# Another plan of tiles, other tap shares and another instruction order in a local-attention and MoE kernel

## The chip, the cores and the metric

The kernel runs on one core of a Trainium2 chip. The metric is device time in microseconds of one execution. Engines: TensorE (PE; PEld is its weight load), VectorE (DVE), ScalarE (ACT), GpSimd (POOL), and SyncE (SP), which only issues DMAs here.

## The reference

The input is `x` (8 x 3584 tokens of 192 numbers) and a weight generator of 8 heads with 7 taps per token. Each token's output of the first part is a softmax-weighted sum of itself and the six tokens before it; the second part routes each of the 28,672 tokens to one of 8 experts and applies that expert's two-layer network.

```python
w = softmax(weight_gen, over the 7 taps)
x1 = einsum('bshk,bskhg->bshg', w, windows_of_7(x_pad))      # attention, 8 heads of 24
logits = x1 @ w_gate                                         # 8 experts
e = argmax(logits)
for each expert e:                                           # tokens of that expert
    h  = relu(x1[mask] @ w1[e])                              # 192 -> 1024
    ye = h @ w2[e]                                           # 1024 -> 192
    out[mask] = softmax(logits)[e] * sigmoid(x1 @ w_output_gate)[e] * ye
```

## The kernel before, in words

**Units.** The tokens are worked in 32 units of 896 (128 partitions x 7). For each unit the front half loads `x` and `w` (`load_steps`, line 651), makes the softmax of the taps (`softmax_steps`, 676), forms the seven products x times w and adds them, scales the sum and splits it into two f16 parts (`sum_steps`, 822), transposes it (a DMA transpose into `gt` from unit 5 on), takes the gate's logits on PE, finds each token's expert and its place within that expert's rows (rank matmuls with `upper` and `ones`, line 905), and scatters the unit's 896 rows into `srtd` in DRAM, sorted by expert: seven indirect DMAs on POOL's queue (`place_steps`, 970).

**Taps.** `TAPS(u)` (1380) gives the first n of the seven products to POOL and the rest to VectorE. Units below `PE_U` = 6 always take `PRO_G` = 4, and PE adds the products up; from unit 6 on `SHARES` decides, or the pattern `POOL`, and VectorE adds the products up in PSUM.

**Rounds and tiles.** `plan_rounds` (28) fixes beforehand how many tiles each unit's round asks for. It counts the rows that have arrived, holds some of them back, and cuts the rest into tiles of T rows: `n = max(0, -(-(left - keep - HOLD(T)) // T))`, at most as the list `EARLY` or `SIZES` says; T is 512 but for the units in `EARLY`. On the chip a round finds for each tile an expert with T sorted rows. The last unit takes all that is left in tiles of 512, 256 and 128 rows. Rows are held back because no expert may yet have T rows of its own.

**A tile's work.** `tile_steps` (1119) waits until a round is filed, that is until all scatters of its units have been issued and are counted as landed, and calls `tile_load` (1141): on SP's queue a load of `meta`, a DMA transpose of the rows into `xT`, and the expert's weights into `wa` (two DMAs) and `wb`. At most `AHEAD` = 2 loaded tiles wait before the last round. `gemm_steps` (1265) then works beats on PE: two of a tile's units of the first matmul (`gemm1_unit`, for 512 rows five matmuls of 512 columns each), and one group of 128 rows of the second (`gemm2_group`, 24 matmuls of 192 columns). ACT and VectorE empty each first-matmul unit (`evac_steps`: `hh`, `hl`), ACT the second one (`out_steps`: `sc` once per tile, `ys`), and POOL scatters `ys` to the output by an indirect DMA per group.

**What sets the order.** Each engine runs its instructions in the order in which the program emits them. `Order.step` (118) emits them by a model: each chain of steps has a time at which its inputs are thought ready, and the chain that can go on first is taken, ties by rank (`RANK_...`, only compared with one another). The model's constants stand at the end: `LAT`, `LAT_S`, `LAT_P`, `LAT_T`, `LAT_R` (from the scan of a unit's ranks to its matmul), `LANDED` (behind a DMA's end), `SLACK`, `SMALL`, `WBX` (when `wb` counts as free again). `FAVOUR` takes tenths of a microsecond off one named chain. The constants change no data, only the emitted order.

**Stirring.** `stir` (502) emits dummy matmuls of 256 columns before a planned gap of PE of at least `STIR[0]` us, `STIR[1]` times the gap in length; it needs a bank of the early sums, which units 0 to 5 use.

Of the kernel before, what the change touches and what calls it, by code (L numbers as in the profile page):

```python
# [27 lines left out]
def plan_rounds(units, every, size):  # L28

    left, rounds = 0, {}  # L30
    for u in range(units):
        left += size
        last = u == units - 1
        if u not in every and not last:
            continue
        subs = []
        for T, keep in SIZES(u, last):
            n = max(0, -(-(left - keep - HOLD(T)) // T))
            while n > 0:
                k = min(n, 8)  # L40
                subs.append((T, k))
                left -= k * T
                n -= k
        if last:
            subs.append((128, (left + NE * TAILK) // 128))
        rounds[u] = subs
    return rounds
# [20 lines left out]
class Chain:  # L68


    def __init__(self, gen, rank, t, engine):
        self.gen, self.rank, self.t, self.engine, self.gate = gen, rank, t, engine, None
        self.favour, self.label = 0.0, ""
        self.slack = EAGER[1] if len(rank) > 1 and rank[0] in EAGER[2] and rank[1] < EAGER[0] else SLACK

# [8 lines left out]
class Order:  # L84
# [7 lines left out]
    def add(self, gen, rank, engine, t=None):  # L92
        c = Chain(gen, rank, self.cur.t if t is None else t, engine)
        c.label = label(gen)
        c.favour = FAVOUR.get(c.label, 0.0)
        self.chains.append(c)
# [60 lines left out]
class Queue:  # L157
# [12 lines left out]
    def __getattr__(self, name):  # L170
        f = getattr(self.engine, name)

        def call(*args, **kwargs):
# [6 lines left out]
            if own is not None:  # L180
                done = self.order.ring.land(self.issued - issue + ARRIVE, own)
                if name == "dma_start_transpose":
                    self.issued = max(self.issued, done - BACK)
                self.moved = max(self.moved, done)
                c.t = max(c.t, done + LANDED)
            return r
# [4 lines left out]
class Paced:  # L191
# [8 lines left out]
    def __getattr__(self, name):  # L200
        f = getattr(self.engine, name)

        def call(*args, **kwargs):
# [4 lines left out]
            if own is not None:  # L208
# [6 lines left out]
                if scatter:  # L215
                    self.landed = self.order.ring.land(self.t - own + 1.6, 0.262) + LANDED
                    held = False
                if held:
                    self.order.port = self.t
                c.t = max(c.t, self.t + self.after)  # L220
                self.order.close(self, args, kwargs, self.t + (LAT_P if self.after == 0.0 else self.after))
            return r
# [29 lines left out]
def vector_cost(name, args, kwargs):  # L252
# [5 lines left out]
    if name == "memset":  # L258
        return 0.03 + (n / 960.0 if n > 8 else 0.0)
    return SMALL + n / 960.0  # L260

# [45 lines left out]
def kernel(ctx: ExitStack, tc: tile.TileContext, x, wg, wgate, wogate, w1, w2, cst, out):  # L307
    nc = tc.nc
    od = Order()
    V = Paced(od, nc.vector, vector_cost, holds=two_in_sbuf)  # L310
# [59 lines left out]
    ps = pp.tile([P, 4096], F32, name="ps")  # L370
    tr_free = [(0.0, ps[:, at : at + 192].bitcast(F16)) for at in TURNS]

# [30 lines left out]
    U = {u: {} for u in range(-RT, NU + 3)}  # L403
# [178 lines left out]
    def weight_steps(stg):  # L582

        for e in range(NE):
# [7 lines left out]
            SP.dma_start(out=st2.rearrange("p (c d) -> p c d", d=D), in_=w2[e].rearrange("(c p) d -> p c d", p=P))  # L592
            od.add(split_steps(e, st1, st2), (RANK_W, e), S)
            if 3 < e < 7:
# [56 lines left out]
    def load_steps():  # L651
        for u in range(1, NU):
            od.named(f"load {u}")
            od.cur.rank = (RANK_X if u <= X_EARLY else RANK_A, -1)
            yield from take(w_free, SP)
            w_load(u)
            U[u]["wt"] = od.cur.t
            od.cur.t = od.now
            od.add(softmax_steps(u), (RANK_A, u, 0), V, U[u]["wt"])
            yield from take(x_free, SP)  # L660
            if u >= XN:
                yield SP, lambda: "zero" in U[u - XN + 1]
            x_load(u)
            U[u]["xt"] = od.cur.t
            od.cur.t = od.now
# [10 lines left out]
    def softmax_steps(u):  # L676

        w4 = wloads[u]
        mxb = f_mx.unsqueeze(2).broadcast_to([P, NV, K])
        yield from take(mx_free, V)  # L680
        V.tensor_reduce(out=f_mx, in_=w4, axis=AX, op=ALU.max)
        yield V
        V.tensor_tensor(out=w4, in0=w4, in1=mxb, op=ALU.subtract)
        yield S
        S.activation(w4, w4, AF.Exp)
        yield V
        V.tensor_reduce(out=f_mx, in_=w4, axis=AX, op=ALU.add)
        yield V
        V.tensor_scalar(f_mx, f_mx, 1e-9, None, op0=ALU.add)
        yield V  # L690
        V.reciprocal(out=f_mx, in_=f_mx)
        yield V

        n = len(TAPS(u)[0])
        V.tensor_tensor(out=w4[:, :, 0:n], in0=w4[:, :, 0:n], in1=f_mx.unsqueeze(2).broadcast_to([P, NV, n]), op=ALU.mult)
        yield V
        U[u]["gw"], U[u]["pool"] = od.cur.t, True
        _, at = yield from take(tw_free, V)
        tw = ps[:, at : at + NV * (K - n)].rearrange("p (v k) -> p v k", k=K - n)
        V.tensor_tensor(out=tw, in0=w4[:, :, n:K], in1=f_mx.unsqueeze(2).broadcast_to([P, NV, K - n]), op=ALU.mult)  # L700
        U[u]["tw"], U[u]["tw_at"], U[u]["tw_k"] = tw, at, n
        mx_free.append(od.cur.t)
        U[u]["wt"] = od.cur.t
        U[u]["soft"] = True
# [40 lines left out]
    def acc_steps(u, taps):  # L745
# [8 lines left out]
        while own or left:  # L754
            yield V, lambda: own or gp
            if own and not (n and gp and gp[0][2] <= od.now + SLACK):
                k = own.pop(0)
# [37 lines left out]
    def add_steps(u, t, tag, kind):  # L795
# [9 lines left out]
        for lo in (0, 512, 1024):  # L805
            hi = min(lo + 512, NV * GD)
            T_.matmul(d["sum"][:, lo:hi], lhsT=cf[:, 0:128], rhs=flat[:, lo:hi], start=(n == 0), stop=(n == K - 1 - PAIRS), skip_group_check=True)
        tap_free[tag].append((od.cur.t + LAT_P, kind))
        if n == 0:
# [3 lines left out]
        if n == K - 1 - PAIRS:  # L813
            d["total"] = d["sum"][:, 0 : NV * GD].rearrange("p (a b) -> p a b", b=GD)
            od.add(sum_steps(u), (RANK_B, u), S, T_.t + LAT_P)

# [5 lines left out]
    def sum_steps(u):  # L822
# [40 lines left out]
        else:  # L863
            od.cur.t += LAT_T
            for j0 in range(0, JS, 2):
# [34 lines left out]
        V.tensor_tensor_scan(out=p3e.rearrange("p e j -> p (e j)"), data0=segs, data1=ohe.rearrange("p e j -> p (e j)"), initial=0.0, op0=ALU.mult, op1=ALU.add)  # L900
        od.cur.t += LAT_R
        yield T_
# [24 lines left out]
    def turn_steps(u, rt, gt, copied):  # L927
        for j in range(JS):
            _, pt = yield from take(tr_free, T_)
            for k in range(3):  # L930
                T_.transpose(out=pt[:, k * 128 : (k + 1) * 128], in_=rt[:, j, k * 128 : (k + 1) * 128], identity=ident)
            od.add(copy_steps(gt[:, j], pt, copied, j), (RANK_B, u), S, T_.t + LAT_P)

# [185 lines left out]
    def tile_steps():  # L1119

        while "all" not in state or queue:
            yield SP, lambda: queue and state["weights"] == NE and len(ahead) < (LATE if "all" in state else AHEAD)
            yield from take(xt_free, SP)
            _, ka = yield from take(wa_free, SP)
            _, kb = yield from take(wb_free, SP)
            T, ti, i, pads, ready, u = queue[0]
            if ready > od.now:
                od.cur.t = ready
                yield SP
            queue.pop(0)  # L1130
            if pads is not None:
                for e in range(NE):
                    row = SP.value_load(pads[0:1, e : e + 1], min_val=0, max_val=DUMMY - P)
                    scattered(SP.dma_start(out=srtd[bass.ds(row, P), :], in_=pad), u)
            d = tile_load(state["t"], T, ti, i, ([n for v, n in state["writers"] if v <= u], [n for v, n in state["writers"] if v > u]), ka, kb)
            d["ready"] = od.cur.t
            state["t"] += 1
            ahead.append(d)
            od.cur.t = od.now
# [17 lines left out]
    def gemm1_unit(hp, d, u, at):  # L1157
# [5 lines left out]
        for i in range(nf):  # L1163
            f = u * nf + i
            b3 = 2048 + f * P
            for q, (wo, k) in enumerate(((f * P, 0), (1024 + f * P, 0), (f * P, 2), (b3, 1), (b3 + 1024, 1))):
                T_.matmul(ps[:, at + i * T : at + (i + 1) * T], lhsT=wa[:, wo : wo + P], rhs=xT[:, k, 0:T], start=(q == 0), stop=(q == 4), skip_group_check=True)
        od.add(evac_steps(d, ps[:, at : at + nf * T], hh[:, 0 : nf * T], hl[:, 0 : nf * T], at, u), (RANK_H,), S, T_.t + LAT_P)

# [9 lines left out]
    def gemm2_group(d, g, at):  # L1179
# [15 lines left out]
        if g == d["G"] - 1:  # L1195
            wb_free.append((T_.t + WBX, d["kb"]))
        od.add(out_steps(d, g, py, at), (RANK_Y,), S, T_.t + LAT_P)

# [121 lines left out]
    with tc.tile_pool(name="stg", bufs=STG, reuse_waits="tile") as stg:  # L1320
        stg_sq = stg
        od.add(weight_steps(stg), (RANK_W, 0), SP)
        while state["weights"] < NE:
# [22 lines left out]
    left = nc.values_load(state["left"][0:1, 0:1], min_val=0, max_val=N // P + NE)  # L1346
# [3 lines left out]
    with tc.For_i(0, left, 1):  # L1350
# [8 lines left out]
        d = tile_load(state["t"], P, ti, 0, ([], []), more, "wb")  # L1359
# [24 lines left out]


RANK_H, RANK_Y, RANK_C, RANK_R, RANK_B, RANK_A, RANK_G = 1, 0, 2, 3, 4, 5, 6
HOLD = lambda T: 6 * T
TAILK = 79
RANK_W = 4.5
LAT = 0.0756  # L1390
LAT_S = 0.2324
LAT_P = 0.3614
LAT_T = 1.8143
LOCK = True
ARRIVE = 1.9478
LANDED = 0.5447
LAT_R = 1.1028
SLACK = 0.0352
SCATTER = 0.987
SMALL = 0.0762  # L1400
EAGER = 0, 0.2, (2, 3, 4)
BACK = 1.0
TURNS = (1536,)
LEAD = 3.3869
STG = 4
# [10 lines left out]
XB = 4  # L1416
MB = 8
PRO_G = 4
POOL = (5,5,4)
SHARES = {18: 5, 11: 4, 28: 4, 20: 4}  # L1420
FAVOUR = {}
PE_U = 6
STIR = 0.8, 0.5
GIVE = 1
RANK_X = 2.5
X_EARLY = 3
RANK_GATE = 4.5
FIRST_G = ()
DEFER = 4
WBX = 3.3548  # L1430
PAIRS = 0
TURN_SP = True
GT = 1
TR_U = 5
EARLY = {2: ((256, 0),), 4: ((384, 0),), 5: ((384, 0),), 6: ((384, 0),)}
EVERY = {*range(99)}
MANUAL = ("SP", "DVE", "PE", "Activation", "Pool")

# [17 lines left out]
```

## Time and profile before

| | us |
|---|---|
| median of 3 runs | 1220.73 (1212.9, 1220.73, 1223.78) |
| the profiled execution | 1223.71 |
| span of its instructions | 1222.0 |
| mean granted TensorE clock | 0.978 of full |
| TensorE busy | 1120.0 |
| VectorE busy | 955.9 |
| POOL busy | 841.5 |
| ScalarE busy | 616.6 |

The span is the time from the first to the last instruction of one execution. The trace names instructions by what they write and read: `gap` and `vap`, `vt` are products of taps on POOL and on VectorE, `srtd<-rt,posi` is a scatter of a unit's rows, `out_dram<-ys,meta` one of results, `ps<-xT,wa` the first matmul of a tile, `ps<-wb,hh` and `ps<-wb,hl` the second, `ps<-gm,gt` the logits. Line 207 is a helper's line that nearly all instructions share; SPq is SyncE's queue.

### The profile page before, as it was taken

How to read it: one execution, taken by the hardware profiler on the slowest of the kernel's cores; microseconds unless marked ns; L12 is line 12 of the kernel's file. 1: busy time of each engine (PE TensorE's matmuls, PEld its weight loads, DVE VectorE, ACT ScalarE, POOL GpSimd, SP SyncE). 2: the span in 40 equal slices, each digit the busy share in tenths (PEclk: the TensorE clock that was granted, in tenths of full speed). 3: DMA queues.
4: the chain of work that ended last, by engine and by line, in shares of the span. 5: the costliest groups of instructions: out<-in, count | busy, mean ns of one | idle time of the engine just before them, and what ended most of it. 6: DMA issues, size and time to landing. Idle time of an engine off the chain costs nothing.

```text
span 1222.0 us, 27128 instructions
## 1 busy us (share of the span) xinstructions
PE 1120.0 (92%) x9693; PEld 812.1 (66%) x9693; DVE 955.9 (78%) x1874; ACT 616.6 (50%) x1300; POOL 841.5 (69%) x620
## 2 busy tenths in 40 slices
PE   8987686899979999999999998899999999999897
PEld 4544375677657666666666666676666666798697
DVE  7999696999999979998999989899998653333231
ACT  4986553455555545455555544455544434434342
POOL 6678783777898868887888877678888554322122
PEclk9999898999989999999999999899999999999999
DMA  8989699998697979799799969887979696599992
GB/s 280 285 276 299 194 287 268 215 270 235 172 264 176 260 225 232 164 250 233 192 244 249 253 163 246 235 212 197 236 193 195 192 270 196 165 292 244 321 292 84
DMA packets 294952, 282.77 MB, mean 231 GB/s; under 512 B 229222, under 2 KB 254423, under 8 KB 294816
## 3 DMA queue, kind: packets, MB, share of 16 engines
q1 hardware_dynamic: 272976, 236.54, 73.0%
q0 software_dynamic: 21696, 44.30, 12.5%
q8 instruction: 76, 1.25, 0.4%
q14 instruction: 60, 0.49, 0.1%
q10 hardware_dynamic: 144, 0.20, 0.1%
HBM read 174.77 MB, written 60.28 MB: 192 GB/s over the span
## 4 chain that ended last, share of the span: by engine, by line
PE 58%; DVE 17%; DMA 9%; issue 8%; POOL 5%; ACT 1%; SPq 1%; another core or an unknown queue 0%; POOLq 0%; DVEq 0%; ACTq 0%
PE ps L207 58%; DVE ps L207 9%; DVE hl L207 4%; DMA wa<-wd 4%; POOL srtd L207 3%; DMA srtd<-rt,posi 2%; POOL gap L207 1%; DVE vt L207 1%; SPq L175 1%; DMA gt<-rt 1%; DMA meta<-srtd 1%; DVE rt L207 1%; POOL out_dram L207 1%; DVE lz L207 1%; DMA w<-in_wg_dram 1%
## 5 line engine op out<-in xcount | busy, mean ns | idle before, releaser
L207 PE MATMUL ps<-xT,wa 128*128 128x512 f16 (+3 forms) x2440 | 491.1, 350 | 42.5 <-DMA wa<-wd 12.8
L207 PE MATMUL ps<-wb,hh 128*128 128x192 f16 x3648 | 473.5, 247 | 8.2 <-ACT ys L207 4.4
L207 PE MATMUL ps<-wb,hl 128*128 128x192 f16 x1824 | 450.1, 247 | 1.4 <-issue 1.4
L207 DVE SCALAR_TENSOR_TENSOR hl<-ps,hh 128x512 f16<-128x512 f32 (+1 forms) x470 | 305.2, 666 | 172.0 <-ACT hh L207 124.0
L207 POOL TENSOR_TENSOR gap<-x,w 128x1344 f32<-128x1344 f32 x145 | 379.4, 2624 | 43.2 <-issue 14.8
L207 POOL DMA_INDIRECT out_dram<-ys,meta x220 | 218.4, 993 | 243.2 <-ACT ys L207 176.1
L207 PEld LDWEIGHTS <-wa 128*128 128x128 f16 x2440 | 226.8, 99 | 229.0 <-issue 47.7
L207 PEld LDWEIGHTS <-hh 128*128 128x128 f16 x3648 | 332.5, 98 | 53.7 <-issue 15.9
L207 ACT ACTIVATE hh<-ps 128x512 f16<-128x512 f32 (+1 forms) x470 | 267.7, 582 | 177.6 <-PE ps L207 147.9
L207 POOL DMA_INDIRECT srtd<-rt,posi x224 | 230.2, 1028 | 85.2 <-issue 57.8
L207 ACT ACTIVATE ys<-ps,sc 128x192 f32<-128x192 f32 x228 | 95.8, 420 | 288.4 <-PE ps L207 180.1
L207 DVE TENSOR_TENSOR ps<-ps,gap 128x1344 f32<-128x1344 f32 x121 | 187.9, 1553 | 0.4
L207 PEld LDWEIGHTS <-hl 128*128 128x128 f16 x1824 | 179.3, 98 | 0.9 <-issue 0.6
L207 DVE SCALAR_TENSOR_TENSOR rt<-ps,sx,rt 128x448 f16<-128x448 f32 x64 | 57.6, 910 | 7.4 <-DMA srtd<-rt,posi 2.5
L207 PE MATMUL ps<-xT,late 128*128 128x128 f16 (+2 forms) x560 | 59.9, 263 | 3.7 <-DMA late<-wd 3.7
L207 PE MATMUL ps<-gap,cf 128*128 128x512 f32 x144 | 60.7, 559 | 0.0
L207 DVE TENSOR_TENSOR ps<-ps,vt 128x1344 f32<-128x1344 f32 x35 | 54.4, 1555 | 0.0
L207 DVE TENSOR_TENSOR vt<-x,ps 128x1344 f32<-128x1344 f32 x35 | 54.1, 1545 | 0.1
L207 PEld LDWEIGHTS <-late 128*128 128x128 f16 x560 | 40.2, 98 | 16.5 <-DMA late<-wd 3.9
L207 ACT ACTIVATE rt<-ps 128x1344 bf16<-128x1344 f32 x32 | 41.3, 1291 | 17.2 <-DVE ps L207 9.5
L207 ACT ACTIVATE rt<-ps,sx 128x1344 f16<-128x1344 f32 x32 | 44.2, 1380 | 11.4 <-DVE sx L207 8.2
L207 PE MATMUL ps<-gm,gt 128*128 128x32 f16 x672 | 28.1, 177 | 20.1 <-ACT gt L207 10.4
(121 smaller groups left out, 809.2 us busy)
## 6 DMA issues: line engine op xcount, KB each, us to landing
wb<-wd SPq DMA_DIRECT2D x75, 768.5 KB
wa<-wd SPq DMA_DIRECT2D x61, 768.0 KB
x<-in_x_dram SPq DMA_DIRECT2D x32, 672.0 KB
late<-wd SPq DMA_DIRECT2D x14, 768.0 KB
wa<-wd SPq DMA_DIRECT2D x61, 128.0 KB
w<-in_wg_dram SPq DMA_DIRECT2D x32, 196.0 KB
wd<-wpb SPq DMA_DIRECT2D x8, 768.5 KB
st<-in_w_dram SPq DMA_DIRECT2D x8, 768.0 KB
```

Source lines behind the costliest of these rows:

```text
L175: r = f(*args, **kwargs)
L207: r = f(*args, **kwargs)
```

## The change

Three functions get one edit each. `plan_rounds` takes the held rows from a table, `load_steps` and `tile_steps` get an added time that is zero. All else is constants: the table of held rows (2816 in place of 3072 for 512-row tiles, 1408 in place of 1536 for 256), the tap shares, the ranks and model constants, two favours, the stirring, and an entry for unit 3 in `EARLY`.

```diff
-            n = max(0, -(-(left - keep - HOLD(T)) // T))
+            n = max(0, -(-(left - keep - HOLDS[T]) // T))
...
-            od.add(softmax_steps(u), (RANK_A, u, 0), V, U[u]["wt"])
+            od.add(softmax_steps(u), (RANK_A, u, 0), V, U[u]["wt"] + (W_LATE if u > PE_U else 0.0))
...
-            d["ready"] = od.cur.t
+            d["ready"] = od.cur.t + T_LATE
...
-HOLD = lambda T: 6 * T
+HOLDS = {128: 768, 256: 1408, 384: 2304, 512: 2816}
 TAILK = 79
-RANK_W = 4.5
+RANK_W = 4.718
 LAT = 0.0756
 LAT_S = 0.2324
-LAT_P = 0.3614
-LAT_T = 1.8143
+LAT_P = 0.384
+LAT_T = 1.85
 LOCK = True
 ARRIVE = 1.9478
-LANDED = 0.5447
-LAT_R = 1.1028
-SLACK = 0.0352
+LANDED = 0.434
+LAT_R = 0.851
+SLACK = 0.038
 SCATTER = 0.987
-SMALL = 0.0762
+SMALL = 0.073
 EAGER = 0, 0.2, (2, 3, 4)
 BACK = 1.0
+W_LATE = 0
+T_LATE = 0.0
...
-POOL = (5,5,4)
-SHARES = {18: 5, 11: 4, 28: 4, 20: 4}
-FAVOUR = {}
+POOL = (5, 5, 5, 4)
+SHARES = {11: 4, 28: 5, 20: 5, 2: 3, 4: 4, 29: 5, 6: 5, 23: 4, 1: 3, 24: 5, 27: 5, 9: 5, 0: 3}
+FAVOUR = {'evac 21 2': 0.4, 'exp 19': -0.1}
 PE_U = 6
-STIR = 0.8, 0.5
+STIR = (0.37, 0.49)
 GIVE = 1
-RANK_X = 2.5
+RANK_X = 2.124
 X_EARLY = 3
-RANK_GATE = 4.5
+RANK_GATE = 4.275
 FIRST_G = ()
 DEFER = 4
-WBX = 3.3548
+WBX = 3.58
...
-EARLY = {2: ((256, 0),), 4: ((384, 0),), 5: ((384, 0),), 6: ((384, 0),)}
+EARLY = {2: ((256, 0),), 4: ((384, 0),), 5: ((384, 0),), 6: ((384, 0),), 3: ((384, 0),)}
```

## Rows read from the trace of the kernel before

**Rows 1.** The page, busy time of the engines; the chain's shares by engine.
```profile
PE 1120.0 (92%) x9693; PEld 812.1 (66%) x9693; DVE 955.9 (78%) x1874; ACT 616.6 (50%) x1300; POOL 841.5 (69%) x620
...
PE 58%; DVE 17%; DMA 9%; issue 8%; POOL 5%; ACT 1%; SPq 1%; another core or an unknown queue 0%; POOLq 0%; DVEq 0%; ACTq 0%
```

**Rows 2.** Busy time by stretch: us, engines (instructions), granted clock, DMA share, GB/s.
```profile
320.00:520.00 200.00, 185.54 (x1588) 129.58 (x1586) 186.06 (x346) 101.32 (x219) 168.25 (x120) 0.97 0.85 218
520.00:690.00 170.00, 163.23 (x1412) 115.98 (x1411) 157.01 (x319) 92.12 (x198) 145.60 (x103) 0.99 0.90 235
690.00:1010.00 320.00, 299.27 (x2560) 209.88 (x2558) 271.52 (x560) 155.45 (x341) 237.79 (x186) 0.98 0.86 217
1010.00:1146.00 136.00, 131.94 (x1411) 110.84 (x1408) 44.38 (x65) 54.05 (x111) 40.51 (x42) 1.00 0.81 230
...
343.00:349.00 6.00, 0.32 (x5) 0.22 (x4) 5.80 (x20) 1.83 (x7) 5.63 (x4) 0.70 1.05 279
866.00:928.00 62.00, 60.01 (x507) 42.33 (x505) 58.36 (x110) 32.25 (x71) 54.46 (x39) 1.00 0.84 206
```

**Rows 3.** The chain before 349 us; SP's queue from 315 us (start, us, what).
```profile
335.50 1.01 POOL out_dram L207
...
343.55 5.29 DMA wa<-wd
...
315.46 0.40 SPq L175 DMA_DIRECT2D meta<-srtd  x1
...
319.61 8.00 SPq L175 DMA_TRANSPOSE gt<-rt  x1
```

**Rows 4.** PE in order of time, from 348 and from 659 us (start, us, what [idle before]).
```profile
348.89 3.97 PE L207 MATMUL ps<-xT,wa 128*128 128x512 f16 x10 [5.68 <-DMA wa<-wd]
...
659.93 2.32 PE L207 MATMUL ps<-xT,wa 128*128 128x512 f16 x10
...
664.07 2.32 PE L207 MATMUL ps<-xT,wa 128*128 128x512 f16 x10
```

**Rows 5.** Loads issued and first scales done, counted from 0 to four moments (ns; first, last start).
```profile
L175 SPq DMA_DIRECT2D meta<-srtd x15: 111/398/423, 143.7 to 340.9; - x15
...
L207 ACT ACTIVATE sc<-meta,wb x15: 278/287/311, 164.2 to 372.2; 128x3 f32<-128x3 f32 x7, 128x2 f32<-128x2 f32 x5, 128x4 f32<-128x4 f32 x3
...
L175 SPq DMA_DIRECT2D meta<-srtd x45: 12/401/708, 143.7 to 874.1; - x45
...
L207 ACT ACTIVATE sc<-meta,wb x45: 278/287/311, 164.2 to 921.9; 128x4 f32<-128x4 f32 x33, 128x3 f32<-128x3 f32 x7, 128x2 f32<-128x2 f32 x5
```

**Rows 6.** POOL in order of time, from 662 us.
```profile
662.91 0.98 POOL L207 DMA_INDIRECT srtd<-rt,posi  x1 [0.30 <-issue]
663.91 2.58 POOL L207 TENSOR_TENSOR gap<-x,w 128x1344 f32<-128x1344 f32 x1
666.66 1.01 POOL L207 DMA_INDIRECT out_dram<-ys,meta  x1 [0.17 <-issue]
```

**Rows 7.** VectorE in order of time, from 660 us.
```profile
660.09 1.55 DVE L207 TENSOR_TENSOR ps<-x,ps 128x1344 f32<-128x1344 f32 x1
661.55 0.69 DVE L207 SCALAR_TENSOR_TENSOR hl<-ps,hh 128x512 f16<-128x512 f32 x1
```

**Rows 8.** POOL's products (lowest/median/highest ns); the rank matmuls (busy, mean | idle before).
```profile
L207 POOL TENSOR_TENSOR gap<-x,w x145: 2555/2579/3798, 9.6 to 942.4; 128x1344 f32<-128x1344 f32 x145
...
L207 PE MATMUL ps<-p,upper 128*128 128x8 f16 x32 | 5.6, 175 | 10.2 <-DVE p L207 7.3 <-DVE ps L207 2.0 <-DVE ex_x L207 0.6
```

**Rows 9.** The dummy matmuls (ns; first, last start); PE in order of time, from 126 us.
```profile
L511 PE MATMUL ps<-pad,ident x110: 269/273/421, 4.3 to 145.8; 128*128 128x256 f16 x110
...
126.33 0.24 PE L207 MATMUL ps<-gm,gt 128*128 128x32 f16 x3 [4.76 <-ACT gt L207]
...
126.58 4.17 PE L207 MATMUL ps<-gap,cf 128*128 128x512 f32 x6
...
133.39 2.47 PE L207 MATMUL ps<-gap,cf 128*128 128x512 f32 x6
```

## The prediction

> **What bounds the kernel now.** I read the busy line of the page first, then the chain, then busy time by stretch, and only then single waits. TensorE is busy 92% of the span and carries 58% of the chain; VectorE is second in both, with 78% and 17% [rows 1]. An average says little here, so the stretches decide. From 320 to 520 us PE is busy 185.5 of 200 us, from 520 to 690 163.2 of 170, from 690 to 1010 299.3 of 320, and from 1010 to 1146 131.9 of 136 [rows 2]. What PE computes is fixed: the change keeps the number and size of the tiles (below). So time can go only out of PE's idle time (14.5 + 6.8 + 20.7 = 42.0 us from 320 to 1010) and out of the half clock. In those stretches the mean granted clock is 0.97, 0.99 and 0.98 [rows 2]; with two levels, 1.2 and 2.4 GHz, the cycles missing are 0.03 x 200 + 0.01 x 170 + 0.02 x 320 = 14.1 us. Some 56 us in all, 4.6% of the span, is what the best order of this middle could win.
>
> The work of a sorted tile is regular: one beat is ten matmuls of 512 columns and 24 of 192, and the next beat starts 664.07 - 659.93 = 4.14 us later [rows 4]. A 512-row tile has four beats, 16.6 us. A unit brings 896 rows, seven beats, 29.0 us. POOL is as full: per unit it issues seven scatters of a unit's rows and, at 1.75 tiles, seven scatters of results, each 0.98 us with 0.30 us in front (0.17 after a tap), and four or five taps of 2.58 us [rows 6]. With five taps that is 5 x 2.58 + 14 x 0.98 + 5 x 0.17 + 9 x 0.30 = 30.2 us, with four 27.7. So PE and POOL need nearly the same time for a unit, and the coupling between them is the load of a tile: it may start only when the last scatter of its round has landed.
>
> That coupling can be seen. Before the tile loaded at 340.89 the chain runs through POOL's queue (out_dram, 335.50) into the weight load of 5.29 us [rows 3]. PE waits 5.68 us for it, and its first ten matmuls then take 3.97 us instead of 2.32 because the clock is at half [rows 4]. In 343 to 349 PE is busy 0.3 of 6 us while DVE has 5.8 and POOL 5.6 [rows 2]: the front half runs on, and TensorE starves.
>
> **The change part by part.** *Held rows.* I work the plan from its formula. Up to unit 7 both plans are alike: 5 tiles of 256 rows at unit 2, then 3, 2 and 2 of 384 at units 4, 5 and 6, and one of 512 at unit 7. The entry for unit 3 gives nothing: 2304 rows are there, 2304 are held back. From unit 8 the old plan gives 1, 2, 2, 2 tiles over four units, the new one 2, 2, 1, 2, and so on to unit 30, where both stand at 53. The last unit gives the same 22. So 75 tiles and 29,184 rows stay, and the last stage stays; only one tile of each fours' first unit and one of its second come a unit earlier (units 8, 12, 16, ..., 28 and 9, 13, ..., 29). Counted against 1.75 tiles a unit, the worst point of the old supply is 0.75 tile behind (after unit 8), that of the new one 0.25 (after unit 10): half a tile, 8.3 us of PE, is gained. The wait at 348.89 is for tile 15 of the count [rows 5], the first tile of unit 9's round; by the new plan unit 8's round brings it, whose rows were out one unit sooner. I count the whole wait and the half clock behind it: 5.7 + (3.97 - 2.32) = 7.3 us less. It stays won, since the 8.3 us lead is more than the 7.3. Bounds: 0 if the next tile starves instead, and all idle time of 320 to 690, 14.5 + 6.8 = 21.3 us, if the lead covers every wait there. I take 7.3, the wait that has a row.
>
> The moved loads are not free on SP's queue: each is five DMAs (meta, xT, two of wa, wb), whose issue took 319.61 - 315.46 = 4.2 us for the tile before, with the transposes of a unit's gt, 8.00 us, behind them [rows 3]. Two loads in one unit make the gt of that unit, and with it its logits, ranks and scatters, up to 4.2 us later; two units on one load fewer gives it back. I take 0, since the rows so delayed are wanted a unit later, and 4.2 if POOL runs dry of scatters.
>
> What is late next? From 690 on nothing of the supply: tile 45 is loaded at 874.1 and its first scale comes at 921.9, 48 us later, against 31 us (340.9 to 372.2) for the starved tile 15 [rows 5]. Seventeen us of backlog lie there, so earlier tiles win nothing more.
>
> *Shares of taps.* Entries for units 0 to 5 are dead, as the prologue takes four. From unit 6, units 7, 15, 19 and 31 go from five POOL taps to four; 8, 14, 17, 20, 26, 28 and 29 from four to five: 121 becomes 124. VectorE loses three products, 1.46 us each from start to next start [rows 7], 4.4 us; its adds stay. POOL gains 3 x (2.58 + 0.17 - 0.30) = 7.4 us. For VectorE two of the units (28, 29) lie where it leads, but PE idles only 2.0 us from 866 to 928 [rows 2], so the gain is between 0 and 2.0; I take 1.0. POOL's extra is +1 tap over units 10 to 21 and two after. The former is covered by the half-tile lead, the latter by the 17 us of backlog; I take 0, and 7.4 if the cover is gone.
>
> The row for POOL's product has 2555, 2579 and 3798 ns as lowest, median and highest [rows 8]: hardly one was held up. The Trainium skill (Perfetto Trace Analysis, section Optimizing Scalar/DVE Operations) warns that GpSimd and DVE share an SBUF read port, so that moving work between those two might not help. By the row the move is worth the 1.0 us above; by that rule, if each moved tap held VectorE for its 2.58 us instead of the 1.46 it saves, it would cost 3 x 1.12 = 3.4 us on VectorE and the sum below would be 4.4 us higher. The measured median, 1% over the lowest, speaks for the row.
>
> *Order.* RANK_W, RANK_X and RANK_GATE keep their places between the whole ranks and to one another: 0. W_LATE and T_LATE are zero. The two favours move one evacuation and one exponential by tenths: within 0.4 us either way, 0 taken. LAT_R falls 0.25 us and LANDED 0.11, so the planner puts a unit's rank matmul, and a tile's work, earlier into PE's queue, where everything behind waits for a late head. The 32 rank matmuls have 10.2 us of idle before them, 7.3 in three waits for VectorE's scan [rows 8]. If all 32 waited 0.25 us longer it would be 8.0; as a refit may as well take such waits away, the other end is -10.2. I take +1.5, six of them. The other constants (SLACK, SMALL, LAT_P, LAT_T, WBX) shift by hundredths to tenths on either side and go into the same bounds.
>
> *Stirring.* Dummy matmuls now fill planned gaps from 0.37 us instead of 0.8; there are 110 now, the last at 145.8 [rows 9], because they need the early sums' banks. At 126.33, after 4.76 us of idle, six f32 matmuls take 4.17 us instead of 2.47 [rows 9]. Keeping the clock there saves 1.7 us; I take that. Bounds: +0.5 if dummies stand in the way, -3.4 for two such places.
>
> Sum: -7.3 - 1.0 + 0 + 1.5 - 1.7 = -8.5 us. The profiled execution took 1223.7 us (span 1222.0), 3.0 over the median of the three runs; from it the sum gives 1215.2, and on the scale of the median 1220.7 - 8.5 = **1212.2 us**.
>
> **Rivals.**
> A, the forecast: the starved wait goes, the rest stays, 1205 to 1218. For it: the waits have rows. Chance 0.37.
> B, more than one wait goes: ahead by half a tile, PE is no longer held by the supply anywhere in 320 to 690. Its 21.3 us of idle and 7.7 us of missing clock there make 29; with a quarter left for heads of the queue like the rank matmuls, 22 go: 1199. Against: one wait alone shows a load as its cause there. Chance 0.27.
> C, nothing: the front half is paced by POOL (30.2 us with five taps against PE's 29.0 and the logits), PE reaches the next tile 7 us sooner and waits there. Only -1.0 + 1.5 - 1.7 is left: 1219.5. For it: 168.3 of 200 us busy plus the gaps in POOL's row from 320 to 520 [rows 2]. Chance 0.18.
> D, slower: POOL's queue. The new shares put five taps into seven units in a row (24 to 30), 30.2 us each; scatters are late by 7.4 us, tiles with them, and the backlog has gone, so PE waits again where it did not. With three starved waits, each followed by 1.65 us at half clock, 7.4 + 5.0 = +12.4: 1233. It decides once the time from load to first scale after 690 falls from 48 to about 31 us. Against: 17 us of backlog. Chance 0.18.
>
> **How the numbers follow.** About 1%, 12 us, is what a measurement of this kernel tells from no change (its three runs span 11): the bounds are 1208.5 and 1232.9. Faster: nearly all of B and a quarter of A, 0.37. Slower: most of D, 0.15. The same: the rest, 0.48. The range goes from about B with its last quarter gone too (1220.7 - 29 = 1192; I put 1193) to D, 1233; what lies beyond is under 2 in 10.
>
> **What would show it.** Right: no wait of 5 us before the 15th tile's first matmuls, the 15th load about 20 us sooner, unchanged counts of matmuls, POOL's products 148 instead of 145, PE's idle time from 320 to 520 down from 14.5 to about 8, and more than 110 dummies. Wrong: another load wait of like size after 350 (C), load to first scale near 31 us after 690 (D), or PE idle below 10 us from 320 to 690 (B). The forecast fails if waits at the head of PE's queue, which only the new order sets, change by more than the 7.3.

## The result and the profile after

The changed kernel takes 1205.3 us in the median (1203.84 to 1211.96, 4 runs) against 1219.07 us (1212.9 to 1223.78, 4 runs). The ratio is 0.989, 95% interval 0.985 to 0.9931: 1.1% faster, with an interval that reaches to both sides of the 1% bound, from which on the forecast counted a kernel as faster (chance 0.37; "the same" had 0.48). The forecast was 1212.2 in a range of 1193 to 1233; of its rivals only A (1205 to 1218) holds the time, at its edge. The profiled execution took 1204.23 us, 19.5 us less than the one of before; its median-to-median distance is 13.8, so about 6 us of what the two traces show beside one another is the luck of two executions.

The page after, to be laid beside [rows 1]:

```profile
PE 1112.7 (93%) x9670; PEld 810.6 (67%) x9670; DVE 947.9 (79%) x1873; ACT 615.3 (51%) x1300; POOL 850.3 (71%) x623
...
PE 64%; DVE 15%; issue 5%; DMA 5%; POOL 4%; ACT 2%; another core or an unknown queue 1%; SPq 1%; POOLq 0%; DVEq 0%; ACTq 0%
```

TensorE's share of the chain rose from 58% to 64%, VectorE's fell from 17% to 15%. POOL's busy time rose by 8.8 us, VectorE's fell by 8.0. Now the stretches of [rows 2], with two earlier ones; the two lines on top are of the kernel before, the rest of the changed one:

```profile
90.00:160.00 70.00, 52.15 (x285) 29.66 (x283) 56.73 (x102) 38.81 (x73) 56.93 (x31) 0.93 0.79 250
160.00:320.00 160.00, 139.37 (x1295) 110.11 (x1293) 143.56 (x312) 80.79 (x192) 112.52 (x83) 0.96 0.93 242
...
90.00:160.00 70.00, 54.39 (x303) 31.79 (x302) 54.36 (x103) 41.12 (x77) 60.69 (x34) 0.88 0.83 251
160.00:320.00 160.00, 135.44 (x1258) 107.47 (x1257) 143.28 (x310) 79.74 (x191) 110.98 (x81) 0.94 0.94 243
320.00:520.00 200.00, 192.08 (x1683) 136.48 (x1681) 187.27 (x362) 106.30 (x228) 170.44 (x121) 1.00 0.89 233
520.00:690.00 170.00, 159.09 (x1357) 111.94 (x1356) 152.12 (x307) 87.06 (x192) 137.74 (x100) 0.99 0.82 217
690.00:1010.00 320.00, 307.71 (x2680) 218.95 (x2678) 275.21 (x565) 161.57 (x354) 257.09 (x196) 1.00 0.87 223
...
343.00:349.00 6.00, 6.00 (x58) 4.72 (x56) 6.00 (x8) 2.70 (x6) 5.35 (x5) 1.00 0.91 231
```

From 320 to 520 us PE does 192.1 us of work instead of 185.5 and the clock is whole; from 690 to 1010 it does 307.7 instead of 299.3. From 520 to 690 it does 4.1 us less. In 343 to 349, where it stood still, it is busy throughout. From 160 to 320 the clock stands at 0.94 (0.96 before) and PE idles 24.6 us: that stretch is no better than before, when PE did 139.4 us of work in it. PE's idle time from 320 to 520 is 7.9 us, the 8 that the forecast named as a sign; where that lead went shows below. The loads and first scales of [rows 5], same tiles:

```profile
L175 SPq DMA_DIRECT2D meta<-srtd x15: 382/398/424, 140.4 to 325.0; - x15
...
L207 ACT ACTIVATE sc<-meta,wb x15: 279/287/303, 161.8 to 368.0; 128x3 f32<-128x3 f32 x7, 128x2 f32<-128x2 f32 x5, 128x4 f32<-128x4 f32 x3
...
L175 SPq DMA_DIRECT2D meta<-srtd x45: 3/403/691, 140.4 to 852.5; - x45
...
L207 ACT ACTIVATE sc<-meta,wb x45: 279/287/314, 161.8 to 904.9; 128x4 f32<-128x4 f32 x33, 128x3 f32<-128x3 f32 x7, 128x2 f32<-128x2 f32 x5
```

Tile 15 is loaded at 325.0 instead of 340.9, and its first scale comes 4.2 us sooner; tile 45's comes at 904.9 instead of 921.9, 17.0 us sooner. So two thirds of the 19.5 us are won between these two tiles, after the wait that the forecast counted. The tiles between say where. The first scales counted to tile 34 and to tile 37, before and after, and the busy time of about that stretch, before and after:

```profile
L207 ACT ACTIVATE sc<-meta,wb x34: 278/287/311, 164.2 to 715.3; 128x4 f32<-128x4 f32 x22, 128x3 f32<-128x3 f32 x7, 128x2 f32<-128x2 f32 x5
...
L207 ACT ACTIVATE sc<-meta,wb x34: 279/287/314, 161.8 to 714.5; 128x4 f32<-128x4 f32 x22, 128x3 f32<-128x3 f32 x7, 128x2 f32<-128x2 f32 x5
...
L207 ACT ACTIVATE sc<-meta,wb x37: 278/287/311, 164.2 to 781.4; 128x4 f32<-128x4 f32 x25, 128x3 f32<-128x3 f32 x7, 128x2 f32<-128x2 f32 x5
...
L207 ACT ACTIVATE sc<-meta,wb x37: 279/287/314, 161.8 to 764.9; 128x4 f32<-128x4 f32 x25, 128x3 f32<-128x3 f32 x7, 128x2 f32<-128x2 f32 x5
```

```profile
715.00:781.00 66.00, 56.52 (x458) 38.26 (x456) 54.66 (x105) 29.86 (x65) 41.97 (x35) 0.92 0.98 236
...
714.00:765.00 51.00, 50.16 (x444) 35.71 (x442) 48.91 (x96) 28.14 (x63) 44.21 (x33) 1.00 0.90 226
...
739.74 0.18 PE L207 MATMUL ps<-p,upper 128*128 128x8 f16 x1 [2.94 <-DVE p L207]
```

At tile 34 the changed kernel is only 0.8 us ahead: what it had won by then (9.1 us at tile 23, 509.0 against 518.1) is lost again. At tile 37 it is 16.5 us ahead, and it stays so. Between these tiles PE idles 9.5 us before and 0.8 after, and the clock before is 0.92 of full, which is 5.3 us of missing cycles. The longest of the waits there is that of a rank matmul for VectorE's `p` (the last line, of the kernel before). The last places are the dummies and POOL's products (for [rows 8, 9]), and the rank matmuls:

```profile
L511 PE MATMUL ps<-pad,ident x87: 269/273/421, 4.3 to 142.2; 128*128 128x256 f16 x87
...
L207 POOL TENSOR_TENSOR gap<-x,w x148: 2555/2579/3800, 9.5 to 943.7; 128x1344 f32<-128x1344 f32 x148
```

```profile
L207 PE MATMUL ps<-p,upper 128*128 128x8 f16 x32 | 5.7, 177 | 6.7 <-DVE p L207 5.6 <-DVE hl L207 0.9
```

POOL's products are three more and as quick as before (2579 ns median). The dummies are fewer, 87 for 110, although they may now fill shorter gaps; the forecast had named more than 110 as a sign. The rank matmuls wait 6.7 us instead of 10.2.

### The profile page after: what moved, and what is told of

The parts are those of the page before. It is cut to its first block, busy times and chain, and to the rows that moved or that the text cites. A ratio compares the mean times of both kernels' runs of the same rounds, so it can differ in the third digit from the quotient of the medians.

```text
span 1202.5 us, 27079 instructions
## 1 busy us (share of the span) xinstructions
PE 1112.7 (93%) x9670; PEld 810.6 (67%) x9670; DVE 947.9 (79%) x1873; ACT 615.3 (51%) x1300; POOL 850.3 (71%) x623
## 4 chain that ended last, share of the span: by engine, by line
PE 64%; DVE 15%; issue 5%; DMA 5%; POOL 4%; ACT 2%; another core or an unknown queue 1%; SPq 1%; POOLq 0%; DVEq 0%; ACTq 0%
PE ps L207 64%; DVE ps L207 8%; DVE hl L207 3%; DMA srtd<-rt,posi 2%; POOL gap L207 2%; DMA wa<-wd 2%; POOL srtd L207 2%; SPq L175 1%; DVE vt L207 1%; DVE rt L207 1%; POOL out_dram L207 1%; DMA x<-in_x_dram 1%; ACT hh L207 1%; DVE w L207 1%
## 5 line engine op out<-in xcount | busy, mean ns | idle before, releaser
L207 PE MATMUL ps<-xT,wa 128*128 128x512 f16 (+3 forms) x2480 | 505.4, 352 | 34.8 <-DMA wa<-wd 13.2
L207 POOL TENSOR_TENSOR gap<-x,w 128x1344 f32<-128x1344 f32 x148 | 387.3, 2621 | 38.8 <-issue 15.9
L207 PEld LDWEIGHTS <-wa 128*128 128x128 f16 x2480 | 232.1, 99 | 225.3 <-issue 33.2
L207 DVE TENSOR_TENSOR ps<-ps,gap 128x1344 f32<-128x1344 f32 x124 | 192.9, 1555 | 2.5 <-POOL gap L207 1.8
L207 DVE TENSOR_TENSOR ps<-ps,vt 128x1344 f32<-128x1344 f32 x32 | 49.8, 1556 | 0.0
L207 PE MATMUL ps<-vap,cf 128*128 128x512 f32 (+1 forms) x108 | 46.2, 567 | 3.6 <-DVE vap L207 3.6
L207 DVE TENSOR_TENSOR vt<-x,ps 128x1344 f32<-128x1344 f32 x32 | 49.5, 1545 | 0.1
L207 PEld LDWEIGHTS ps<-gap,cf 128*128 128x128 f32 x144 | 26.5, 194 | 25.4 <-issue 23.8
L207 DVE TENSOR_TENSOR ps<-x,ps 128x1344 f32<-128x1344 f32 x26 | 40.2, 1547 | 0.1
```

The source lines that it names most:

```text
L207: r = f(*args, **kwargs)
```

## The experiments

All ratios are to the kernel before, run beside it on the same chip. The first eight ran on chips where before takes 1219.0 to 1219.8 us, the last four on a faster chip, where it takes 1183.7. Times don't go across. That ratios do is taken for granted and not shown: of the kernels here only the one before ran on both kinds. The profiled execution of each kernel is one of its runs, and need not be a middle one. The theories: S, the supply of tiles, is the forecast's; T and T2 give the gain to the tap shares, alone or only in the new order; O gives it to the emitted order as a whole; V and E ask which units' shares count.

**One part alone: the held rows on the kernel before.**

```diff
-            n = max(0, -(-(left - keep - HOLD(T)) // T))
+            n = max(0, -(-(left - keep - HOLDS[T]) // T))
...
-HOLD = lambda T: 6 * T
+HOLDS = {128: 768, 256: 1408, 384: 2304, 512: 2816}
```

> The kernel before with only the table of held rows of the change (2816 and 1408). Theory S (supply: tiles half a tile earlier end the wait before the 15th tile): 0.6% faster than the kernel before, ratio 0.991 to 0.997, the 15th tile's load near 325 us in place of 341 and no wait over 3 us on a weight load from 320 to 690 us. Theory O (the whole order: each new order has its own waits, and the change's own set happens to be good): ratio anywhere from 0.99 to 1.01, with the wait before the 15th tile gone and others of the same sum in its place. Theory T (tap shares): ratio 1.000.

Measured: 0.9981 (0.995 to 1.0012), 2.3 us less, which is not clear of none. The 15th load is indeed sooner, 327.7 us:

```profile
L175 SPq DMA_DIRECT2D meta<-srtd x15: 16/393/478, 142.9 to 327.7; - x15
```

But the wait has not gone, it has moved. PE in order of time, then the chain of waits ahead of it:

```profile
424.96 4.16 PE L207 MATMUL ps<-xT,wa 128*128 128x512 f16 x10 [5.62 <-DMA wa<-wd]
```

```profile
413.05 1.57 DVE ps L207
...
415.12 0.69 DVE hl L207
...
416.91 0.42 SPq L175
417.49 1.46 SPq L175
419.15 5.38 DMA wa<-wd
```

PE waits 5.62 us for weights at 425 us, and the ten matmuls behind take 4.16 us, the clock being 0.56 of full from 425 to 429.2 us: the very price of [rows 4], four tiles later. The chain leads from VectorE's work into SP's load, then 5.38 us of weights. I read it so: the front half is not ahead of PE, so tiles that come sooner are eaten sooner, and the next one is late. That is rival C's mechanism, with VectorE and not POOL in the chain.

**The held rows taken back from the changed kernel.**

```diff
-HOLDS = {128: 768, 256: 1408, 384: 2304, 512: 2816}
+HOLDS = {128: 768, 256: 1536, 384: 2304, 512: 3072}
```

> The changed kernel with the old held rows (3072 and 1536). Theory S: most of the gain is lost, ratio to the kernel before 0.994 to 1.000, with a wait of about 5 us on the 15th tile's weights again. Theory O: anywhere from 0.985 to 1.005. Theory T: 0.989, as the changed kernel.

Measured: 0.9908 (0.9879 to 0.9936). Nearly all of the gain stays. The wait on the 15th tile's weights, which theory S wanted back, does not come back either: from 320 to 690 us PE has no wait for a weight load in this kernel, nor in the changed one. Theory S has fallen from both sides: the held rows are worth about 0.2% in either order, and the intervals allow none.

**The shares alone on the kernel before.**

```diff
-POOL = (5,5,4)
-SHARES = {18: 5, 11: 4, 28: 4, 20: 4}
+POOL = (5, 5, 5, 4)
+SHARES = {11: 4, 28: 5, 20: 5, 2: 3, 4: 4, 29: 5, 6: 5, 23: 4, 1: 3, 24: 5, 27: 5, 9: 5, 0: 3}
```

> The kernel before with only the new tap shares. Theory S: ratio 0.998 to 1.002, as three taps are worth 1 us at most. Theory T: near 0.992, with VectorE's idle time and PE's idle time from 690 to 1010 us down as in the changed kernel. Theory O: 0.99 to 1.01.

Measured: 0.9999 (0.997 to 1.0027). Taken by itself that says the shares do nothing. Its busy time by stretch says more:

```profile
160.00:320.00 160.00, 135.08 (x1228) 106.94 (x1226) 136.03 (x305) 77.65 (x187) 106.45 (x79) 0.93 0.88 237
320.00:520.00 200.00, 181.88 (x1565) 127.11 (x1563) 183.04 (x340) 99.18 (x215) 166.57 (x118) 0.97 0.86 227
520.00:690.00 170.00, 163.80 (x1413) 116.62 (x1412) 161.01 (x323) 92.33 (x200) 142.26 (x103) 0.99 0.85 227
690.00:1010.00 320.00, 309.04 (x2688) 219.22 (x2686) 274.32 (x569) 159.23 (x353) 257.23 (x197) 1.00 0.82 219
```

From 690 to 1010 PE does 309.0 us of work, 9.8 more than before [rows 2], more even than in the changed kernel. What it won there it lost ahead: from 160 to 690 it does 480.8 us against 488.1 before, and its tile 34 comes 13.6 us later. (This profiled execution took 1212.3 us, 6 less than the median of 1218.2; that of before took 3 to 5 us more than its medians. So the trace shows this kernel too well by some 10 us.) One of the places is a wait that before did not have here:

```profile
396.28 4.02 PE L207 MATMUL ps<-xT,wa 128*128 128x512 f16 x9 [6.27 <-DMA wa<-wd]
```

**The order alone on the kernel before.**

```diff
-LAT_P = 0.3614
-LAT_T = 1.8143
+LAT_P = 0.384
+LAT_T = 1.85
...
-LANDED = 0.5447
-LAT_R = 1.1028
-SLACK = 0.0352
+LANDED = 0.434
+LAT_R = 0.851
+SLACK = 0.038
...
-SMALL = 0.0762
+SMALL = 0.073
...
-STIR = 0.8, 0.5
+STIR = (0.37, 0.49)
...
-WBX = 3.3548
+WBX = 3.58
```

> The kernel before with only the new model constants (LAT_P, LAT_T, LANDED, LAT_R, SLACK, SMALL, WBX) and the new stirring. Theory S: 1.000 to 1.003. Theory O: this edit alone rewrites the order of all engines, so 0.99 to 1.01, and the waits from 320 to 1010 us lie in other places than in the kernel before. Theory T: 1.000.

Measured: 1.0005 (0.9974 to 1.0035). Nothing by itself. So none of these three parts alone carries the gain, and the question was what two of them do together.

**The shares taken back from the changed kernel.** The lines of the third edit, reversed.

> The changed kernel with the old tap shares (121 taps on POOL in place of 124). Theory T2 (the shares carry the gain, but only in the new order): ratio to the kernel before 0.997 to 1.003. Theory O (no part carries it; each order has its own waits, about +-0.5% from one to the next): anywhere from 0.985 to 1.005. Theory S (supply) has fallen with the two runs on the held rows.

Measured: 0.9994 (0.9965 to 1.0024). All of the gain is gone; its interval and that of the changed kernel don't meet. With the new constants the shares are worth 0.9994 - 0.989 = 1.0%, some 12.7 us. The trace was taken of the slowest of this kernel's 12 runs (1225.2 us, median 1217.8), so beside the changed kernel's it shows more than the 12.7:

```profile
690.00:1010.00 320.00, 297.15 (x2545) 209.11 (x2543) 272.56 (x562) 153.61 (x341) 239.56 (x182) 0.98 0.82 215
```

From 690 to 1010 PE does 297.2 us of work against 307.7 with the new shares. The waits of that stretch (us in total, times, longest), first with the old shares, then of the changed kernel:

```profile
POOL out_dram L207 <- ACT ys L207: 31.7, 16, 4.2
...
PE ps L207 <- DVE hl L207: 9.6, 11, 2.6
...
PE ps L207 <- ACT ys L207: 7.5, 6, 4.1
```

```profile
POOL out_dram L207 <- ACT ys L207: 18.8, 10, 2.6
...
PE ps L207 <- ACT ys L207: 4.3, 3, 2.3
...
PE ps L207 <- DVE hl L207: 1.4, 3, 0.8
```

PE's waits for a bank to be emptied by VectorE (`hl`) or ScalarE (`ys`) fall from 17.1 to 5.7 us. POOL's waits for results to scatter fall from 31.7 to 18.8 us: POOL had been waiting for results of the second matmul, it was not the engine that led there. This pair is the widest of all; the table below has the others.

**Two orders with no purpose, and the favours.** Three kernels ask how much of a result is the accident of one emitted order. The changed kernel without favours, and with one nanosecond less in the model for each VectorE instruction; the kernel before with the same:

```diff
-FAVOUR = {'evac 21 2': 0.4, 'exp 19': -0.1}
+FAVOUR = {}
```
```diff
-SMALL = 0.073
+SMALL = 0.072
```
```diff
-SMALL = 0.0762
+SMALL = 0.0752
```

> The changed kernel without the two favours (tenths of a microsecond on one evacuation and one exponential). The prediction's term: 0, ratio 0.989. Theory O: the order behind tile 21 (the favoured evacuation, near 490 us) is written anew, so the ratio lies anywhere from 0.985 to 1.000 and the times at which tiles begin differ from those of the changed kernel only after about 480 us.

> The changed kernel with SMALL 0.072 in place of 0.073, one nanosecond of the model's time per VectorE instruction: a new order with no purpose. Theory O: ratio between 0.985 and 1.003, and another set of waits; the gain may shrink by half or more. If the new constants and shares are good in themselves (theory T2), the gain stays: 0.987 to 0.992.

> The kernel before with SMALL 0.0752 in place of 0.0762: the same purposeless reorder of the kernel before. Theory O: 0.993 to 1.007. Theory T2: 1.000 within 0.2%. If before was itself a picked order, more likely slower than faster.

Measured: 0.9893 (0.9861 to 0.9925), 0.989 (0.9848 to 0.9931), and 1.0135 (1.0085 to 1.0184). The changed kernel keeps its time in three orders; the kernel before loses 1.35% by one nanosecond in a constant. In its reorder PE works less in three of these four stretches, all but 320 to 520 us:

```profile
160.00:320.00 160.00, 133.75 (x1207) 103.85 (x1206) 137.40 (x303) 76.75 (x183) 112.81 (x81) 0.95 0.95 248
320.00:520.00 200.00, 186.89 (x1601) 130.17 (x1599) 179.09 (x340) 100.40 (x219) 156.60 (x114) 1.00 0.79 205
520.00:690.00 170.00, 162.57 (x1430) 116.16 (x1429) 160.13 (x323) 93.17 (x202) 144.53 (x103) 1.00 0.88 237
690.00:1010.00 320.00, 294.06 (x2496) 206.79 (x2495) 270.02 (x546) 152.42 (x338) 236.99 (x180) 0.97 0.79 207
```

In 690 to 1010 it does 294.1 us of work, the least of all. One reading is that the time of before is that of a well-fitting order, and that an edit made to it alone pays for leaving it, which would be why the shares alone gave nothing. It is not shown: one such reorder of before was run, and the new constants alone, which write the order anew as well, cost nothing (1.0005).

The ten profiles from the chips where before takes 1219 us, in three measures: PE's busy us from 690 to 1010; the us from tile 34's first scale to tile 54's, which holds the same tiles in each kernel, as a stretch fixed in time does not; and PE's waits for `hl` and `ys` from 690 to 1010, in us.

| tap shares | kernels | PE busy | tile 34 to 54 | waits |
|---|---|---|---|---|
| old | before; with the new held rows; with the new order; changed with old shares; before, reordered | 299.3, 297.3, 304.2, 297.2, 294.1 | 366.4, 361.2, 358.5, 364.0, 374.3 | 8.4, 11.7, 7.6, 17.1, 10.8 |
| new | changed; with the old held rows; before with new shares; changed without favours; changed, reordered | 307.7, 304.6, 309.0, 308.0, 304.8 | 349.6, 355.7, 347.1, 353.7, 356.5 | 5.7, 11.1, 4.8, 5.3, 6.5 |

By the first two measures no kernel with the old shares reaches one with the new, though the closest pairs are 0.4 and 2.0 us apart, and some of the kernels share most of their order. The means of PE's work are 298.4 and 306.8, 8.4 us apart; those of tile 34 to 54 are 364.9 and 352.5, 12.4 us apart, about the whole gain of the changed kernel. They are not quicker there only for being late: three of the kernels with the new shares reach tile 34 within 1 us of before (715.3). So in these ten the shares act in this stretch, whatever the held rows and the constants; whether it shows in the time depends on what an order loses ahead of tile 34. The waits for `hl` and `ys` differ by 4.4 us in the mean (11.1 and 6.7), and their ranges overlap: they are a part of it at most.

**Which units' shares.** On the faster chip: the changed kernel with the old shares from unit 24 on, with the old shares in units 7 to 23, the reordered kernel before with the new shares, and the changed kernel with five POOL taps everywhere. (`SHARES` lists the units with four; the others have five. In the first, second and fourth the lines shown stand in place of the changed kernel's `POOL` and `SHARES`.) From unit 6 on POOL makes 121 products with the old shares and 124 with the new, 122 and 123 in the first two kernels, 130 in the last.

```diff
+POOL = (5,)
+SHARES = {7: 4, 11: 4, 15: 4, 19: 4, 23: 4, 26: 4, 28: 4, 29: 4}
```

> The changed kernel with the old shares in units 24 to 31 (26, 28 and 29 take four POOL taps again, 31 five). Theory V (VectorE leads the last eight units of the front half; their three products taken off it are the gain): the stretch from tile 37 to tile 54 grows by about 7 us, from 299 to 306, and the ratio to the kernel before is 0.994 to 0.998. Theory E (the earlier units' new rhythm carries it): 0.989 to 0.991.

```diff
+POOL = (5,)
+SHARES = {8: 4, 11: 4, 14: 4, 17: 4, 20: 4, 23: 4, 31: 4}
```

> The changed kernel with the old shares in units 7 to 23 and the new ones from 24 on. Theory V: most of the gain stays, 0.989 to 0.993, and tile 37 to tile 54 stays near 299 us. Theory E: 0.996 to 1.000.

```diff
-SMALL = 0.0762
+SMALL = 0.0752
...
-POOL = (5,5,4)
-SHARES = {18: 5, 11: 4, 28: 4, 20: 4}
+POOL = (5, 5, 5, 4)
+SHARES = {11: 4, 28: 5, 20: 5, 2: 3, 4: 4, 29: 5, 6: 5, 23: 4, 1: 3, 24: 5, 27: 5, 9: 5, 0: 3}
```

> The kernel before with SMALL 0.0752 and the new tap shares. If the shares are worth 1% in any order and the kernel before was only a lucky order of the old ones, the ratio to the kernel before falls from 1.0135 to about 1.000 to 1.004. If the shares need the new constants, it stays above 1.008.

```diff
+POOL = (5,)
+SHARES = {}
```

> The changed kernel with five POOL taps in all units from 6 on (130 on POOL in place of 124): six more products off VectorE, 8.8 us, and 14.7 us more on POOL. If VectorE is what holds the front half, the gain grows: 0.983 to 0.989. If POOL is by now as full (30.2 us a unit by the prediction's count against the 30.1 us at which units follow each other), it turns: 0.992 to 1.003, with VectorE's and PE's waits on POOL's products and on weight loads back.

Measured: 0.9893 (0.9867 to 0.992), 0.9895 (0.9868 to 0.9921), 0.986 (0.9836 to 0.9884), and 0.9952 (0.9928 to 0.9975).

The first two contradict both theories: with either half of the new shares the ratio is that of the changed kernel, where V and E each gave the gain to one half. So it is not the three late products that count, nor the number: the first kernel moves one product net, the second two. This holds if ratios go across, for neither the changed kernel nor the one with all the old shares ran on this chip. From tile 37 to 54, which V named, the two take 290.2 and 289.4 us, no 7 us apart. The third goes further than foreseen: the reorder that cost before 1.35% has, with the new shares, the lowest ratio of the study. It has the old held rows and the old constants but one, so the shares need no new constants; and yet, one nanosecond away, the same shares on the kernel before gave 0.9999. So the worth of the shares in one order is anything from 0.0 (kernel before) over 1.0 (new constants) to 2.7% (reordered before, across two chips). That the third kernel beats the changed one is not shown: it ran on another chip, and the two intervals overlap. Of the nine kernels with other than the old shares eight stand at 0.9952 or below, of the five with the old ones none below 0.998.

The fourth turns, as the second of its two cases said. POOL's waits from 320 to 690 us with five taps everywhere, then of the kernel with the old early shares; below them two waits of VectorE and PE with five everywhere:

```profile
POOL srtd L207 <- issue: 24.9, 82, 0.5
POOL out_dram L207 <- issue: 10.9, 53, 0.3
POOL out_dram L207 <- ACT hh L207: 3.9, 16, 0.5
```

```profile
POOL out_dram L207 <- ACT ys L207: 7.1, 9, 1.9
POOL gap L207 <- issue: 5.1, 3, 2.7
```

```profile
DVE ps L207 <- POOL gap L207: 6.2, 10, 1.2
...
PE ps L207 <- DMA wa<-wd: 3.1, 2, 1.6
```

With five everywhere POOL has left little but its short gaps in front of the indirect DMAs; the waits for results (`ys`), 7.1 us in the other kernel, are down to 0.2. VectorE now waits 6.2 us for POOL's products, of which the other kernel lists none, and PE 3.1 us for weights (0.7 there). That fits a full POOL, as the count of 30.2 us per unit had it, and 0.6% are given back. It does not prove it: the third kernel, the lowest of all, keeps POOL as busy from 320 to 520 (175.0 us, 175.5 here).

## Why the prediction came out right, and where not

The direction held, the size was low (8.5 us forecast, 13.4 by the ratio), and the time lies in the range. The reason given for it was wrong: 7.3 of the 8.5 us were put on a part that is worth about nothing, and the part that carries the gain was put at 1.0. That the number came near is luck; two terms of the sum changed places.

- **Held rows, "I count the whole wait and the half clock behind it: 5.7 + (3.97 - 2.32) = 7.3 us less. It stays won".** This step failed. The runs show 0.2% in both orders, about 2 us, with intervals that allow none. The 15th load came sooner and its load wait vanished, as forecast; in the kernel before with this part alone another of 5.62 us stood up at 425 us, and in the changed kernel with the old held rows the wait does not come at all. In the changed kernel the lead is down to 0.8 us at tile 34. The mistake, as I read the chain at 425 us, was to take the supply of tiles as a plan with 1.75 tiles a unit: what counts is when a unit's rows are out, and the front half was no faster.
- **Shares, "the gain is between 0 and 2.0; I take 1.0".** This is the term that was mis-sized: 12.7 us with the new constants, nothing on the kernel before, and 12.4 us from tile 34 to tile 54 over all ten profiles. I had bounded it by PE's 2.0 us of idle in one window where VectorE leads the chain. That window was the wrong place: the changed kernel gains 15.7 us on the one before between tiles 34 and 37, ahead of it. Short waits of PE for banks that VectorE and ScalarE empty are shorter with the new shares, but by 4.4 us in the mean, and in the kernel before they were 8.4 in all. Only 4.4 us of VectorE's work was moved by the forecast's count, and with either half of the shares one or two products; that the gain exceeds it is measured, and which change of rhythm does it is open.
- **POOL's extra, "I take 0".** Nothing speaks against it for three taps; the run with nine shows a cost.
- **Rival D (POOL's queue) and the shared read port.** Neither came. The time from load to first scale at tile 45 is 52.4 us, not 31. POOL's products kept 2579 ns in the median, as in [rows 8], and moving three of them helped by 1% with the new constants. So the warning of the Trainium skill (Perfetto Trace Analysis, section Optimizing Scalar/DVE Operations), that moving work between VectorE and GpSimd might not help, was not borne out there; on the kernel before the move gave nothing.
- **Order and stirring, +1.5 and -1.7.** Together -0.2 forecast, +0.6 measured with an interval from -3.2 to +4.3. The sum is not contradicted, its parts are: the rank matmuls' idle time fell by 3.5 us (10.2 to 6.7) in the changed kernel, and the dummies fell to 87. From 90 to 160 us the clock is 0.88 (0.93 before), so there is no sign that the 1.7 us of clock was won. The stirring need not be the cause: with the old stirring and 110 dummies the kernel with the new held rows has 0.87 there.
- **Ranks, favours, dead entries at 0.** Right for the favours: without them the ratio is 0.9893. The ranks keep their places in every comparison of the program, the shares of units 0 to 5 are never read, and the entry for unit 3 leaves the plan as it is; no run took these out.
- **What I did not price.** How much one order may differ from the next: a nanosecond in a constant cost before 1.35%, 16.5 us, more than the +8.0 that I had as the bound of the order, and there as the cost of one constant.

Not settled: what in the new shares does it. They have five taps in three of every four units up to unit 23 and in all of units 24 to 30, as tiles too come in a rhythm of four units; before, it was two of three. The half-and-half kernels tell that it is not the count of taps moved, but not which rhythm, and were run on the other chip. Nor was the kernel with all the old shares reordered in the new constants, so that some of its 1.0% may be the accident of one order.

## What to carry to other kernels

Where engines run in an order written beforehand, test a part from both ends: alone on the old kernel and taken out of the new one. Here three parts looked worthless on the old kernel, and taking one of them out of the new one took the whole gain. Before believing a difference of 1%, move the order by a change that means nothing, and see how far the time goes. And compare two traces by when the same tile is reached, not by busy time in stretches fixed in time: here a lead of 9 us at tile 23 was lost again by tile 34, and the gain that lasted came in the three tiles after it.

## What the runs showed of the hardware that I had not expected

The same kernel before takes 1219 us on one chip and 1183.7 on another, 2.9% less. The waits without a visible cause differ with it. Those of the changed kernel on a slower chip, then of the kernel with the old early shares on the faster:

```profile
PEld L207 <- issue: 80.0, 127, 5.5
...
ACT ys L207 <- remote: 20.8, 5, 7.3
```

```profile
PEld L207 <- issue: 33.1, 74, 1.6
```

On the slower chip PE's weight loads stand 80.0 us in all for no reason that the profile shows, and ScalarE 20.8 us for a releaser that the profile calls "remote"; on the faster the first is 33.1 us, and no "remote" wait is listed. These are not the same kernel, but the others agree: the ten profiles from slower chips have 79.5 to 111.1 us of the first, and "remote" waits in each, the four from the faster one 29.8 to 38.5 us, and "remote" waits in none. What it is that stands there was not tried.
